# Attention then a three-way max feed-forward on one core: transposing one more group by DMA, moving copies and loads, spreading pieces, and cutting the last output tile

## The chip, the cores and the metric

The kernel runs on one core of a Trainium2 chip. The metric is the device time of one execution in microseconds (us). Runs of a kernel are compared by their medians.

The engines: PE (TensorE) multiplies matrices into PSUM; PEld is its loading of weights; DVE (VectorE), ACT (ScalarE) and POOL (GpSimd) work elementwise; SP (SyncE) issues DMAs. POOL issues DMAs too. Each engine executes its own instructions in order and waits on semaphores for the others.

## The reference

q, k, v are (8, 12, 448, 64) in float32: 8 batches, 12 heads, 448 tokens. The four weights are 768 x 768.

```python
scores = scale * np.matmul(q, k.transpose(0, 1, 3, 2))
m = np.max(scores, axis=-1, keepdims=True)
e = np.exp(scores - m)
attn = e / (np.sum(e, axis=-1, keepdims=True) + np.exp(-m) + 1e-09)
x = (attn @ v).transpose(0, 2, 1, 3).reshape(8 * 448, 768)
h = np.maximum(np.maximum(x @ w1, x @ w2), x @ w3)
out = h @ w_out                      # (3584, 768), float32
```

The kernel takes exp of the scaled scores without subtracting the maximum, which turns the extra term of the denominator into 1.

## The kernel before

**Groups.** The 12 heads of a batch are three groups of four heads, two pairs each: 24 groups i in all (line 88). Groups 0 to 2 (batch 0) are computed in two halves of the query columns, "E" (256) and "O" (192): parts n = 0 to 5 (lines 499 to 545). From group 3 on, the loop of line 556 takes a whole group in three visits.

**Scores and exp.** A group has seven units (line 249). `scores` (line 260) computes a unit as 64x64 matmuls into a buffer `stp` and has ACT write exp of it into `e_buf` (line 294). Visits take the units (0, 1), (2, 3) and (4, 5, 6). The buffers `stp`, the accumulators `avp` of attention times V, and, where the call says so, the PE transposes' output share the pool `ps_s`, which has three buffers used in turn (line 79). Feed-forward pieces use `ps_b`, two buffers.

**K and Q transposed.** Scores need K and Q with the head dimension on the partitions. Groups below `PE_QK` (line 55) are transposed by PE: `transpose_pe` (line 172) does one pair, 11 blocks of 128x128, and one copy for K and one or two for Q take them out of PSUM on the engines that the call names (AC is ACT, DV is DVE). Groups from `PE_QK` on are transposed by two crossbar DMAs (a DMA that transposes) on SP's queue (`transpose_dma`, line 207), at the start of group i - 2; then `shift_q` (line 216) on POOL moves half blocks with four copies. KT and QT have three buffers each, so the DMA for group i waits until the scores of group i - 3 are done.

**V and loads.** `load_qk` (line 91) and `load_v` (line 108) issue loads from POOL, which turn float32 into float16; the raw tiles have four buffers. `prep_v` (line 354) copies V into the layout of the matmul with three copies, on DVE or POOL. For groups below `PE_QK`, `load_qk` also clears two columns with DVE (line 98).

**Attention times V.** At visits 0 and 1 of group i, `av` (line 495) multiplies the exp of group i - 1 by V; DVE divides by the sum into `xn` (lines 341 to 352). `x_transpose_pe` or, from group 3 on, a crossbar DMA on SP (line 382) turns xn into `xT`.

**Feed-forward pieces.** A batch's feed-forward is a list of pieces: `up_piece` (line 392; one of three weights, one or two column blocks; DVE copies the first product into hT and takes the maximum with the next two) and `out_piece` (line 418; half the width of an output tile of 128 tokens, scaled by DVE; after the second half two DMAs on SP's queue write 64 rows each). Each piece has a cost in PE columns. `fill(cols)` (line 467) adds to a credit and emits pieces while the credit is positive. In the parts, `UPE` (line 493) is given at four places of parts 3 to 5; in the groups, `share(n)` (line 551) is the cost that is left over the visits until the next batch's pieces arrive, in equal parts.

**The end.** After the last group come its attention times V, a crossbar transpose of its x, the pieces that remain, and then the whole last batch's 26 pieces (lines 597 to 602).

Of the kernel before, what the change touches and what calls it, by code (L numbers as in the profile page):

```python
# [14 lines left out]
ts = bass.ts  # L15
# [6 lines left out]
def kernel(  # L22
# [29 lines left out]
    scale = 1.0 / math.sqrt(D)  # L52


    PE_QK = 6
    NEB = 2
    NV = 3

# [295 lines left out]
    def prep_v(i, eng):  # L354
        t = raw[i].pop("v")
        vx, vt = v_buf[i % NV], vt_buf[i % NV]
        eng.tensor_copy(out=vx[:, :, :, 0:D], in_=t[:, :, 1:4, :])  # L357
        t2 = t.rearrange("p (r h) t d -> p r h t d", r=NP)
        eng.tensor_copy(out=vt[0:HP, :, 0:D], in_=t2[0:HP, :, 0, 4, :])
        eng.tensor_copy(out=vt[HP:P, :, 0:D], in_=t2[HP:P, :, 1, 0, :])  # L360
# [50 lines left out]
        else:  # L411
            nc.vector.tensor_tensor(out=dst, in0=dst, in1=src, op=ALU.max)  # L412

    NH = 2
    NW = DM // NH
    order = (0, 2, 4, 6, 1, 3, 5)

    def out_piece(bp, t, nh):
        if nh == 0:
            outs[0] = out_pool.tile([128, DM], FP32, tag="o_sb", name="o_sb")  # L420
        o_sb = outs[0]
        op_ps = ps_b.tile([128, 512], FP32, tag="b", name="op_ps")
        for fc in range(NFC):
            nc.tensor.matmul(  # L424
                out=op_ps[:, 0:NW],
                lhsT=hT[bp][:, fc, ts(t, 128)],
                rhs=wout_sb[:, fc, ts(nh, NW)],
                start=(fc == 0),
                stop=(fc == NFC - 1),
            )  # L430
        nc.vector.tensor_scalar(  # L431
            out=o_sb[:, ts(nh, NW)],
            in0=op_ps[:, 0:NW],
            scalar1=1.0 / LAMBDA,
            scalar2=None,
            op0=ALU.mult,
        )
        if nh == NH - 1:
            for half in range(2):
                n = 2 * t + half  # L440
                b = 2 * bp + n // T
                rows = out[b * S : (b + 1) * S].rearrange("(p t) m -> t p m", t=T)
                nc.sync.dma_start(out=rows[order[n % T]], in_=o_sb[half * HP : half * HP + HP])


    UP = NDC * (S + 6)
    OUT = NFC * (NW + 6)
    pieces = []

    def add_up(b, q0, qn, order):  # L450
        w = 1 if qn == S else 2
        for i, f0 in order:
            fcs = tuple(range(f0, f0 + w))
            pieces.append((up_piece, (b, fcs, i, q0, qn), NDC * w * (qn + 6)))

    def add_out(b):
        for t in range(0, 3) if b % 2 == 0 else range(3, 7):
            for nh in range(NH):
                pieces.append((out_piece, (b // 2, t, nh), OUT))

    def add_batch(b):
        add_up(b, 0, S, [(i, fc) for fc in range(NFC) for i in range(3)])
# [27 lines left out]

    parts = [(part, g) for part in "EO" for g in range(NG)]
    PW = {"E": (0, 1), "O": (2, 3), "EO": (0, 1, 2, 3)}
    UPE = 9 * 2 * NDC * (NE + 6) / 12

    def av(i, ej, pr, part):
        av_tail(i, ej, pr, PW[part])
        av_main(i, ej, pr, PW[part])

    for n, (part, g) in enumerate(parts):
        ej = n % NEB  # L500
        pp, pg = parts[n - 1] if n > 0 else (None, None)
        step = UPE if n > 2 else 0
        nxt = g + 1 if part == "E" and g < NG - 1 else None
        scores(g, ej, (0, 1), part)
        if n != 3:
            scores(g, ej, (2, 3), part)
        if n > 0:
            av(pg, 1 - ej, 0, pp)
        if n > 1 and n != 4:
            x_transpose_pe(parts[n - 2][1], parts[n - 2][0])  # L510
        if n == 3:
            av(pg, 1 - ej, 1, pp)
            scores(g, ej, (2, 3), part)
        fill(step)
        if nxt is not None and n > 0:
            transpose_pe(nxt, 0, ps_b, AC, (DV,))
        fill(step)
        scores(g, ej, (4, 5), part)
        scores(g, ej, (6,), part)
        if n == 0:  # L520
            warm(4)
            transpose_pe(nxt, 0, ps_b, DV, (DV,))
        if n == 3:
            x_transpose_pe(pg, pp)
            add_up(0, 0, NE, [(i, f) for i in range(3) for f in (0, 2, 4)])
        if nxt is not None:
            transpose_pe(nxt, 1, ps_b, DV, (DV,))
        if n > 0 and n != 3:
            av(pg, 1 - ej, 1, pp)
        fill(step)  # L530
        if n == 5:
            transpose_pe(3, 1, ps_s, DV, (DV,))
        fill(step)
        if n == 0:
            prep_v(0, DV)
        if n == 1:
            load_weight(2)
        if n == 2:
            load_v(3)
            load_qk(4)  # L540
            load_weight(3)
        if n == 4:
            load_v(4)
            load_qk(5)
            transpose_pe(3, 0, ps_s, DV, (DV,))


    visits = ((0, 1), (2, 3), (4, 5, 6))
    adds = {3 * (3 * b + 4) + 1: b for b in range(1, B - 1)}

    def share(n):

        nxt = min([a for a in adds if a > n], default=3 * NI + 2)
        return left() / (nxt - n)

    for i in range(3, NI):
        ej, pj = (i + 1) % NEB, i % NEB
        first = i == 3
        if i + 2 < NI and i + 2 >= PE_QK:
            transpose_dma(i + 2)  # L560
        if first:
            load_v(5)
            load_qk(6)
        elif i + 2 < NI:
            load_v(i + 2)
            if i + 3 < NI:
                load_qk(i + 3)
        for vi, units in enumerate(visits):
            n = 3 * i + vi
            scores(i, ej, units)  # L570
            if vi < 2:
                av(i - 1, pj, vi, "O" if first else "EO")
            if vi == 1:
# [24 lines left out]
    av(NI - 1, NI % NEB, 1, "EO")  # L598
# [34 lines left out]
```

The softmax here doesn't subtract the row's maximum and nothing guards it: scores larger than these inputs give would overflow.

## Time and profile before

| | |
|---|---|
| median of 8 runs | 343.78 us (343.38 to 344.83) |
| the profiled execution | 343.93 us |
| its span, first to last instruction | 341.9 us |
| PE busy | 329.6 us, 96% of the span |
| DVE, ACT, POOL busy | 189.5, 146.4, 139.4 us |
| granted TensorE clock | 0.998 of full |
| DMA moved | 47.42 MB, mean 139 GB/s |

The span is cut into 40 slices of 8.5 us; a digit is the busy share in tenths:

```
PE   8889988999999999999999999999999999999993
ACT  2773366585444453544453543444453543300000
DMA  7999999999999999999995999979970460133006
```

A view of a stretch gives its length and then each engine's busy time with the number of instructions in brackets: PE, PEld, DVE, ACT, POOL, then the clock, DMA's mean busy share (over 1 where transfers overlap) and GB/s. A line of the timeline is start, length, engine, line of the code, operation, tiles, count, and in brackets the engine's idle time before it with what ended it. Matmuls overlap one another, so a matmul's length is not its cost; the chain of work that ended last gives the net times, and there six matmuls of 448 columns take 1.13 us. A view of DMA issues gives the time from issue to landing. SPq is SP's queue.

### The profile page before, as it was taken

How to read it: one execution, taken by the hardware profiler on the slowest of the kernel's cores; microseconds unless marked ns; L12 is line 12 of the kernel's file. 1: busy time of each engine (PE TensorE's matmuls, PEld its weight loads, DVE VectorE, ACT ScalarE, POOL GpSimd, SP SyncE). 2: the span in 40 equal slices, each digit the busy share in tenths (PEclk: the TensorE clock that was granted, in tenths of full speed). 3: DMA queues.
4: the chain of work that ended last, by engine and by line, in shares of the span. 5: the costliest groups of instructions: out<-in, count | busy, mean ns of one | idle time of the engine just before them, and what ended most of it. 6: DMA issues, size and time to landing. Idle time of an engine off the chain costs nothing.

```text
span 341.9 us, 9746 instructions
## 1 busy us (share of the span) xinstructions
PE 329.6 (96%) x4157; PEld 198.5 (58%) x4157; DVE 189.5 (55%) x418; ACT 146.4 (43%) x174; POOL 139.4 (41%) x247
## 2 busy tenths in 40 slices
PE   8889988999999999999999999999999999999993
PEld 4568767865545655555555655555556655465552
DVE  2565766655456466456556456556556555565552
ACT  2773366585544453543544453543544443300000
POOL 8693541917477172834355168164345000000000
PEclk9999999999999999999999999999999999999999
DMA  7999999999999999999995999979970460133006
GB/s 103 193 207 209 205 200 162 169 124 193 192 165 147 210 206 118 140 141 202 152 124 71 188 214 144 130 108 228 145 115 4 124 125 3 32 77 94 2 18 167
DMA packets 89499, 47.42 MB, mean 139 GB/s; under 512 B 58224, under 2 KB 85872, under 8 KB 89456
## 3 DMA queue, kind: packets, MB, share of 16 engines
q0 software_dynamic: 29392, 22.03, 47.2%
q1 hardware_dynamic: 60064, 24.78, 42.1%
q8 instruction: 32, 0.52, 0.6%
q14 instruction: 11, 0.09, 0.1%
HBM read 44.04 MB, written 11.01 MB: 161 GB/s over the span
## 4 chain that ended last, share of the span: by engine, by line
PE 92%; DVE 2%; ACT 2%; issue 1%; DMA 1%; POOL 0%; ACTq 0%; POOLq 0%
PE p_i L401 48%; PE op_ps L424 16%; PE avp L331 12%; PE stp L274 11%; PE avp L314 2%; PE trT L181 2%; ACT e L294 2%; DMA ld_k<-in_k_dram 1%; DVE QT L170 1%; DVE xn L347 0%; DVE xT L380 0%; PE xtp L374 0%; PE warm L155 0%; POOL ld_q L103 0%; DVE hT L412 0%
## 5 line engine op out<-in xcount | busy, mean ns | idle before, releaser
L294 ACT ACTIVATE e<-stp 128x896 f16<-128x896 f32 (+4 forms) x171 | 144.0, 903 | 144.5 <-PE stp L274 144.4
L401 PE MATMUL p_i<-xT,w 128*128 128x448 f16 (+2 forms) x972 | 173.6, 332 | 0.2
L401 PEld LDWEIGHTS <-w 128*128 128x128 f16 x972 | 89.8, 98 | 68.0 <-issue 5.3
L412 DVE TENSOR_TENSOR hT<-hT,p_i 128x448 f16<-128x448 f16 (+2 forms) x96 | 59.6, 621 | 43.4 <-PE p_i L401 43.2
L219 POOL COPY QT<-QT 64x384 f16<-64x384 f16 (+1 forms) x72 | 40.0, 556 | 101.8 <-DMA QT<-ld_q 80.5
L424 PE MATMUL op_ps<-w,hT 128*128 128x384 f16 x336 | 58.3, 326 | 0.0
L274 PE MATMUL stp<-QT,KT 64*64 64x448 f16 (+2 forms) x756 | 47.8, 338 | 3.4 <-ACT e L294 1.9
L331 PE MATMUL avp<-vx,e 128*128 128x65 f16 x1152 | 45.4, 193 | 0.0
L431 DVE TENSOR_SCALAR o_sb<-op_ps 128x384 f32<-128x384 f32 x56 | 31.0, 556 | 25.4 <-PE op_ps L424 22.4
L424 PEld LDWEIGHTS <-hT 128*128 128x128 f16 x336 | 31.6, 98 | 23.1 <-issue 2.1
L410 DVE CAST hT<-p_i 128x448 f16<-128x448 f32 (+2 forms) x48 | 30.0, 624 | 23.8 <-PE p_i L401 23.6
L331 PEld LDWEIGHTS <-e 128*128 128x128 f16 x1152 | 38.8, 97 | 2.3
L347 DVE TENSOR_TENSOR xn<-avp,rb 128x512 f16<-128x512 f32 (+1 forms) x54 | 34.1, 632 | 1.9
L274 PEld LDWEIGHTS <-KT 64*64 64x64 f16 x756 | 15.8, 105 | 28.2 <-issue 24.2
L341 DVE TENSOR_SCALAR rb<-avp 128x8 f32<-128x8 f32 (+1 forms) x54 | 9.0, 166 | 40.1 <-PE avp L331 40.0
L314 PEld LDWEIGHTS <-e 64*64 64x64 f16 x768 | 14.5, 107 | 9.2 <-DVE QT L170 0.8
L103 POOL DMA_DIRECT2D ld_q<-in_q_dram x24 | 17.7, 737 | 4.1 <-PE avp L331 1.6
L103 POOL DMA_DIRECT2D ld_k<-in_k_dram x25 | 17.9, 716 | 3.2 <-DMA w<-in_moe_w_out_dram 1.5
L357 POOL COPY vx<-ld_v 128x768 f16<-128x768 f16 x20 | 16.4, 819 | 5.2 <-issue 2.7
L314 PE MATMUL avp<-vt,e 64*64 64x65 f16 x768 | 15.7, 193 | 1.4 <-DVE QT L170 0.6
L116 POOL DMA_DIRECT2D ld_v<-in_v_dram x24 | 15.2, 633 | 3.1 <-DMA ld_q<-in_q_dram 1.9
L113 POOL DMA_DIRECT2D ld_v<-in_v_dram x24 | 15.2, 635 | 2.3 <-DVE rb L341 1.6
(33 smaller groups left out, 85.1 us busy)
## 6 DMA issues: line engine op xcount, KB each, us to landing
out_dram<-o_sb SPq DMA_DIRECT2D x56, 192.0 KB, 3.3
ld_v<-in_v_dram POOLq DMA_DIRECT2D x48, 128.0 KB, 5.0
ld_q<-in_q_dram POOLq DMA_DIRECT2D x24, 224.0 KB, 7.5
ld_k<-in_k_dram POOLq DMA_DIRECT2D x23, 224.0 KB, 6.9
w<-in_moe_w_dram POOLq DMA_DIRECT2D x9, 384.0 KB, 9.2
w<-in_moe_w_out_dram POOLq DMA_DIRECT2D x3, 384.0 KB, 10.9
xT<-xn SPq DMA_TRANSPOSE x21, 4.9
QT<-ld_q SPq DMA_TRANSPOSE x18, 6.0
```

Of the source, the lines that this page charges most:

```text
L103: nc.gpsimd.dma_start(out=tiles[nm][:, 1 : NP * T + 1].rearrange("x (r t) d -> x r (t d)", r=NP)[:, p0:p1], in_=src[:, p0:p1],)
L219: eng.tensor_copy(out=t[d0 : d0 + HP, o * 128 : (o + n) * 128], in_=t[s0 : s0 + HP, a * 128 : (a + n) * 128],)
L274: nc.tensor.matmul(out=stp[half * HP : half * HP + HP, par, j * qn : (j + 1) * qn], lhsT=k_block(i, pr, h2, x[half]), rhs=q_cols(i, pr, h2 ...
L294: nc.scalar.activation(out=dst, in_=src, func=AF.Exp, scale=scale)
L314: nc.tensor.matmul(out=ps[half * HP : half * HP + HP, hh, j * D1 : (j + 1) * D1], lhsT=eF[hh * HP : hh * HP + HP, o : o + HP], rhs=vt[hh * ...
L331: nc.tensor.matmul(out=ps[:, hh, j * D1 : (j + 1) * D1], lhsT=eF[:, o : o + 128], rhs=vx[:, 2 * pr + hh, (x[0]), 0:D1], start=False, stop= ...
L347: nc.vector.tensor_tensor(out=xn[i][:, pr, ws[0] : ws[0] + nw].rearrange("p j h d -> p h j d"), in0=acc[:, :, :, 0:D], in1=rb[:, :, 0:nw]. ...
L401: nc.tensor.matmul(out=p_i[:, j * qn : (j + 1) * qn], lhsT=w_sb[i][:, dc, ts(fc, 128)], rhs=xT[b][:, dc, q0 : q0 + qn], start=(dc == 0), s ...
L410: nc.vector.tensor_copy(out=dst, in_=src)
L412: nc.vector.tensor_tensor(out=dst, in0=dst, in1=src, op=ALU.max)
L424: nc.tensor.matmul(out=op_ps[:, 0:NW], lhsT=hT[bp][:, fc, ts(t, 128)], rhs=wout_sb[:, fc, ts(nh, NW)], start=(fc == 0), stop=(fc == NFC - 1),)
L431: nc.vector.tensor_scalar(out=o_sb[:, ts(nh, NW)], in0=op_ps[:, 0:NW], scalar1=1.0 / LAMBDA, scalar2=None, op0=ALU.mult,)
```

## The change

1. `PE_QK` goes from 6 to 5: group 5 is transposed by DMA, shifted by POOL, and its V is copied by POOL.
2. Parts: `UPE` is one whole piece of 3144 columns instead of 2358; it is given once after `add_up` in part 3 and twice each in parts 4 and 5, instead of four times in each. V of group 0 is copied by DVE before the second transpose of part 0 instead of at its end; that transpose's Q is copied out by ACT and DVE. The transposes of group 3 have Q copied out by ACT instead of DVE, and the one in part 5 stands before the `fill`.
3. Groups: the transposes of group 4 stand at visits 0 and 1 of group 3, before the `fill`, and are copied out by ACT; before, they stood at visits 1 and 2 in the middle of the `fill`, copied by DVE.
4. POOL's V copies are those of group i + 1 and stand at the end of group i, ahead of `shift_q(i + 2)`; before, they were those of group i and stood in visit 1. The loads of V for group i + 3 and K, Q for group i + 4 stand at the end of group i behind `shift_q`, from group 4 on; before, V of i + 2 and K, Q of i + 3 stood at the start of group i.
5. `share` counts 2200 columns for attention times V at visits 0 and 1, so that these get fewer pieces and visit 2 more.
6. The last output tile is written as columns of 384, 256 and 128, each with its own two DMAs: both on SP, both on ACT, and one on each.

```diff
-    PE_QK = 6
+    PE_QK = 5
...
-    def out_piece(bp, t, nh):
-        if nh == 0:
+    def out_piece(bp, t, c, w, queues):
+
+        if c == 0:
             outs[0] = out_pool.tile([128, DM], FP32, tag="o_sb", name="o_sb")
+            outs[1] = 0
...
-        if nh == NH - 1:
-            for half in range(2):
...
-                nc.sync.dma_start(out=rows[order[n % T]], in_=o_sb[half * HP : half * HP + HP])
+        if queues is None:
+            return
+        for half in range(2):
...
+            queues[half].dma_start(
+                out=rows[:, outs[1] : c + w], in_=o_sb[half * HP : half * HP + HP, outs[1] : c + w]
+            )
+        outs[1] = c + w
...
     def add_out(b):
+        sy, sc = nc.sync, nc.scalar
         for t in range(0, 3) if b % 2 == 0 else range(3, 7):
-            for nh in range(NH):
-                pieces.append((out_piece, (b // 2, t, nh), OUT))
+            cuts = [(0, NW, None), (NW, NW, (sy, sy))]
+            if b == B - 1 and t == 6:
+                cuts = [(0, NW, (sy, sy)), (NW, 256, (sc, sc)), (NW + 256, 128, (sy, sc))]
+            for c, w, queues in cuts:
+                pieces.append((out_piece, (b // 2, t, c, w, queues), NFC * (w + 6)))
...
-    UPE = 9 * 2 * NDC * (NE + 6) / 12
+    UPE = 2 * NDC * (NE + 6)
...
-        step = UPE if n > 2 else 0
+        step = UPE if n > 3 else 0
...
             transpose_pe(nxt, 0, ps_b, AC, (DV,))
-        fill(step)
         scores(g, ej, (4, 5), part)
         scores(g, ej, (6,), part)
         if n == 0:
             warm(4)
             transpose_pe(nxt, 0, ps_b, DV, (DV,))
+            prep_v(0, DV)
         if n == 3:
             x_transpose_pe(pg, pp)
             add_up(0, 0, NE, [(i, f) for i in range(3) for f in (0, 2, 4)])
+            fill(UPE)
         if nxt is not None:
-            transpose_pe(nxt, 1, ps_b, DV, (DV,))
+            transpose_pe(nxt, 1, ps_b, DV, (AC, DV) if n == 0 else (DV,))
         if n > 0 and n != 3:
             av(pg, 1 - ej, 1, pp)
+        if n == 5:
+            transpose_pe(3, 1, ps_s, DV, (AC,))
         fill(step)
-        if n == 5:
-            transpose_pe(3, 1, ps_s, DV, (DV,))
-        fill(step)
-        if n == 0:
-            prep_v(0, DV)
...
-            transpose_pe(3, 0, ps_s, DV, (DV,))
+            transpose_pe(3, 0, ps_s, DV, (AC,))
...
+    AVC = 2200
+
     def share(n):
...
-        return left() / (nxt - n)
+        rest = range(n, nxt)
+        sums = [AVC if m % 3 < 2 and m < 3 * NI else 0 for m in rest]
+        return max(0, (left() + sum(sums)) / len(rest) - sums[0])
...
-        if first:
-            load_v(5)
-            load_qk(6)
-        elif i + 2 < NI:
-            load_v(i + 2)
-            if i + 3 < NI:
-                load_qk(i + 3)
+        def loads(iv, iq):
+            if iv < NI:
+                load_v(iv)
+            if iq < NI:
+                load_qk(iq)
+
+        if i < 5:
+            loads(i + 2, i + 3)
...
             if vi == 1:
-                prep_v(i, nc.vector if i < PE_QK else nc.gpsimd)
+                if i < PE_QK:
+                    prep_v(i, nc.vector)
...
-            if vi > 0 and i + 1 < PE_QK:
-                fill(per / 2)
-                transpose_pe(i + 1, vi - 1, ps_s, DV, (DV,))
-                fill(per / 2)
-            else:
-                fill(per)
-        if i + 2 < NI and i + 2 >= PE_QK:
+            if vi < 2 and i + 1 < PE_QK:
+                transpose_pe(i + 1, vi, ps_s, AC, (AC,))
+            fill(per)
+        if PE_QK <= i + 1 < NI:
+            prep_v(i + 1, nc.gpsimd)
+        if PE_QK <= i + 2 < NI:
             shift_q(i + 2, nc.gpsimd)
+        if i >= 4:
+            loads(i + 3, i + 4)
```

More of the change, by code (lines that the diff above doesn't have):

```diff
@@ L412, in up_piece @@
             nc.vector.tensor_tensor(out=dst, in0=dst, in1=src, op=ALU.max)
-    NH = 2
-    NW = DM // NH
+    NW = DM // 2
     order = (0, 2, 4, 6, 1, 3, 5)
-    def out_piece(bp, t, nh):
-        if nh == 0:
+    def out_piece(bp, t, c, w, queues):
+        if c == 0:
             outs[0] = out_pool.tile([128, DM], FP32, tag="o_sb", name="o_sb")
+            outs[1] = 0
         o_sb = outs[0]
@@ L424, in out_piece @@
             nc.tensor.matmul(
-                out=op_ps[:, 0:NW],
+                out=op_ps[:, 0:w],
                 lhsT=hT[bp][:, fc, ts(t, 128)],
-                rhs=wout_sb[:, fc, ts(nh, NW)],
+                rhs=wout_sb[:, fc, c : c + w],
                 start=(fc == 0),
@@ L431, in out_piece @@
         nc.vector.tensor_scalar(
[L432 to L435, printed above, removed]
+            out=o_sb[:, c : c + w], in0=op_ps[:, 0:w], scalar1=1.0 / LAMBDA, scalar2=None,
             op0=ALU.mult,
         )
-        if nh == NH - 1:
-            for half in range(2):
-                n = 2 * t + half
-                b = 2 * bp + n // T
-                rows = out[b * S : (b + 1) * S].rearrange("(p t) m -> t p m", t=T)
-                nc.sync.dma_start(out=rows[order[n % T]], in_=o_sb[half * HP : half * HP + HP])
+        if queues is None:
+            return
+        for half in range(2):
+            n = 2 * t + half
+            b = 2 * bp + n // T
+            rows = out[b * S : (b + 1) * S].rearrange("(p t) m -> t p m", t=T)[order[n % T]]
+            queues[half].dma_start(
+                out=rows[:, outs[1] : c + w], in_=o_sb[half * HP : half * HP + HP, outs[1] : c + w]
+            )
+        outs[1] = c + w
     UP = NDC * (S + 6)
-    OUT = NFC * (NW + 6)
     pieces = []
```

## The prediction

> **What bounds the kernel now.** I read the page's busy shares first, then TensorE's (PE) busy time stage by stage, then its waits in order of time.
>
> ```profile
> PE 329.6 (96%) x4157; PEld 198.5 (58%) x4157; DVE 189.5 (55%) x418; ACT 146.4 (43%) x174; POOL 139.4 (41%) x247
> 60.00:100.00 40.00, 40.00 (x608) 25.34 (x606) 23.20 (x52) 23.81 (x29) 23.32 (x42) 1.00 1.23 168
> 34.56:42.03 7.47, 6.88 (x122) 5.79 (x120) 5.12 (x15) 2.71 (x4) 4.04 (x7) 1.00 1.24 204
> 42.03:51.85 9.82, 8.44 (x135) 6.73 (x134) 6.48 (x18) 5.99 (x7) 4.49 (x7) 1.00 1.30 201
> 51.85:61.90 10.05, 9.16 (x181) 7.83 (x180) 6.64 (x18) 5.99 (x7) 3.42 (x7) 1.00 1.25 157
> ```
>
> The last four are a stretch, its length, then PE's busy time. From 60 us on PE has no idle time up to its last matmul near 336.7, so spreading pieces differently there can win nothing: only work taken from PE, idle time before 62 us, and the 5.2 us behind the last matmul can shrink. Group 3 (42.03 to 51.85) has 1.38 us of idle PE, group 4 0.89.
>
> The timeline names the waits; brackets hold the idle time and its releaser:
>
> ```profile
> 46.07 0.33 PE L181 MATMUL trT<-ident,ld_k 128*128 128x128 f16 x3 [0.35 <-ACT e L294]
> 48.34 0.38 PE L274 MATMUL stp<-QT,KT 64*64 64x448 f16 x4 [0.89 <-ACT e L294]
> 58.88 0.38 PE L274 MATMUL stp<-QT,KT 64*64 64x448 f16 x4 [0.89 <-ACT e L294]
> 35.68 0.26 PE L314 MATMUL avp<-vt,e 64*64 64x65 f16 x8 [0.59 <-DVE QT L170]
> ```
>
> The first three have one cause: a group's PE transposes take one of the three `ps_s` buffers just before the visit that wants all three, so its third score unit waits for an exp. They are 2.13 us.
>
> **The change part by part.**
>
> *Group 5 leaves PE (PE_QK 6 to 5).* The chain of waits has each of its two transpose steps (56.87 and 60.36) as "0.61 PE trT L181 x11". Removed: 2 x 0.61 = 1.22 us, in a stretch where PE otherwise works: full gain. DVE also loses four copies. Added are two crossbar transposes on SP's queue and four shift copies on POOL (2.38 us), priced below.
>
> The Trainium skill (VectorE: DVE Perf Modes, "The three transpose paths" and its rules) speaks against this: TensorE if PSUM will do, 390 ns a 128x128 block against 1309 ns for the crossbar. The trace pays 0.61/11 = 55 ns a block on PE and 5.3 us to land a Q transpose of seven blocks. By the page's figure, as an estimate, that would land after 9.2 us and group 5 would be about 3 us late, which would eat most of the change's gain.
>
> *Transposes of group 4 at visits 0 and 1, copied out by ACT.* That removes 0.35 and 0.89 in group 3; group 4, with no PE transposes left, loses its 0.89. ACT takes over four copies in two visits of group 3: K 0.49 and 0.60 (its rows for 384 and 512 columns), Q of 1024 and 896 columns. ACT's Q copy of that width is not shown; ends are 0.60 (512 columns) and 1.03 (its 1024-wide exp); I take 1.0 and 0.9, the nearer row by width. So ACT has 6.4 us of exps plus 3.0 in group 3, 9.4 against about 10.8 of PE (below): covered, but behind the visit-1 exp the second transpose waits about 0.3. Net 2.13 - 0.3 = **1.8 us**; ends 1.0 (ACT's order bites each time) and 2.1.
>
> *Fewer pieces early.* Before, parts 3, 4, 5 run 2, 3, 3 pieces of 1.31 us (rows of 12 matmuls in the chain); now 1, 2, 2, then 1, 1, 2 in group 3. Parts keep 3.3 to 5.6 us of PE work against 2.9 us of exps, so the cover holds and the three pieces move, costing nothing. If it failed, each part would show some 0.5 us of wait. The 0.59 at 35.68 stays: the Q copy before it goes from DVE (0.68) to ACT (1.0), but starts without K's 0.29 ahead.
>
> *V copy ahead at part 0.* DVE's V copies (13.67 to 14.44) move ahead of the last K/Q copies; V landed near 11.5 (issued 5.15 and 5.78, landing 6.0), so nothing new waits. The av matmul at 14.27, which waits for them, comes 0.1 earlier, and score unit 3 0.2 later: 0.1 gained, ends -0.3 and +0.3.
>
> *Loads and POOL's order.* Laid side by side, POOL's order from group 6 on is the same cycle (loads, V copy, shift copies); only the V copy is of the next group. Loads "two groups ahead" stand where they stood. What is new is group 5's shift copies ahead of V6 and QK7's loads. POOL executes in order, so those loads wait for the crossbar transpose of Q5:
>
> ```profile
> 39.09 0.71 POOL L103 DMA_DIRECT2D ld_q<-in_q_dram  x1 [0.40 <-PE avp L331]
> 46.96 0.63 POOL L113 DMA_DIRECT2D ld_v<-in_v_dram  x1 [0.40 <-issue]
> 52.88 1.32 SPq L211 DMA_TRANSPOSE QT<-ld_q  x1
> 54.32 1.65 SPq L211 DMA_TRANSPOSE KT<-ld_k  x1
> 58.32 2.38 POOL L219 COPY QT<-QT 64x384 f16<-64x384 f16 x4 [7.91 <-DMA QT<-ld_q]
> 60.64 0.62 POOL L113 DMA_DIRECT2D ld_v<-in_v_dram  x1
> 70.02 1.50 SPq L211 DMA_TRANSPOSE QT<-ld_q  x1
> ```
>
> Q5 is issued at 39.09 and lands 10.1 us later, 49.2. Its transpose, like that of 52.88, takes 5.3: 54.5. Shift copies end at 56.9; K5's transpose (6.8 at 54.32) ends by 57.4. Group 5's scores come at 61.90 - 1.22 - 1.83 - 0.1 and less one odd piece of 0.99 = **57.8**: in time by half a microsecond. V6 is then issued at 56.9, not 46.96. In before, V7's issue at 60.64 led to Q8's landing at 70.0 (62.56 + 7.4), 9.4 later; so Q7 lands at 65.5 to 66.3. Its transpose takes 5.3 to 7.7 (rows at 52.88 and 70.02): 70.8 to 74.0, shift copies to 73.2 to 76.4; K7's 1.5 later by 6.8 to 8.5. Group 7's scores come at 77.34 - 3.15 = **74.2**. So a wait of 0 to 2.2; I take **0.6**, from the middle of the transposes' rows. Group 8 (shift end before 80.2, scores 87.84) keeps over 3 us, and later groups more.
>
> *V copies of POOL* (0.82 + 0.29 + 0.29): one group earlier, V landed a cycle before; nothing waits. Group 5's moves from DVE to POOL.
>
> *Spreading by AVC.* PE is full there: 0. The bigger remainder at the end (about 19,900 columns, 8.3 us, before 7.5) still covers the last x transpose (2.8 us).
>
> *The end.*
>
> ```profile
> 336.78 0.56 DVE L431 TENSOR_SCALAR o_sb<-op_ps 128x384 f32<-128x384 f32 x1 [0.42 <-PE op_ps L424]
> out_dram<-o_sb SPq DMA_DIRECT2D x56, 192.0 KB, 3.3
> ```
>
> The last matmul ends at T = 336.74. Now: scaling 0.56, two issues on SP at 0.57, landing 2.6 for the last two: T + 3.76. Then 1.4 us to the span's end. After: the 256-column scaling ends near T + 0.13 (0.56 for 384 columns and 0.17 for 8 give 0.42 and, for 128, 0.29). ACT issues its two DMAs, then one of the last two; the third starts at T + 0.17 + 2 x 0.52 = T + 1.2. ACT issues no DMA in this trace; by SP's rows one takes 0.47 to 1.03. Landing of 32 KB is not shown: between 1.8 (2.6 less 0.8, for the 192 KB fewer in flight at the tail's some 230 GB/s) and 2.6; I take 2.2: T + 3.4. **0.35 gained**; ends -1.0 (issues of 1.03) and +1.2 (issues of 0.3, landing 1.8). The extra matmuls cost nothing: 6 x 55 ns and 6 x 109 sum to the 0.97 of one old piece.
>
> The Trainium skill (DMA: Bandwidth & Descriptors, "Rules for kernel authors") calls transfers under 64 KB mostly overhead, and more issuing engines a saving of issue time alone. By its fit (2.0 us plus bytes at 436 GB/s, an estimate) 32 KB lands in 2.1 against 2.45 for 192 KB, a landing gain of 0.35, near my 0.4; the trace's 2.6 agrees with the larger.
>
> *Sum:* 1.22 + 1.83 + 0.1 + 0.35 - 0.6 = **2.9 us**. The profiled execution took 343.93 (span 341.9 plus 2.0): 341.0. It lies 0.15 above the median 343.78, so **340.9**.
>
> **Rivals.**
> 1. *The waits return as ACT waits.* ACT at 9.4 of 10.8 us delays exps instead. For: 0.35 at 46.07 already is ACT. Against: ACT is at 5.99 in both stretches and idles. Gain 1.22 + 0.35 (the end), no wait at group 7 since PE is later: 342.2.
> 2. *Group 7 long late.* The transposes take 7.7 and 8.5 as at 70.02, wait 2.2, perhaps 0.5 at group 5. For: DMA's mean busy share is 1.2 to 1.3 until 77 us. Against: a transpose at 59.30 landed in 3.4. 342.5 to 343.1.
> 3. *Slower than before.* The same chain, POOL held by group 5's shift copies: shift 7 ends at 56.8 plus three landings (Q5's transpose, Q7's load counted from its issue, Q7's transpose). It is in time up to 17.4; from 17.4 + 3.5 + 0.7 = 21.6 the kernel is slower. With three of the long rows, 9.4 + 8.0 + 9.4 = 26.8, 9.4 late: about 349.7. Against: with loads held back, fewer transfers compete just then.
> 4. *It doesn't do what it says.* The load move alone is no new order on POOL; if the PE gain is also eaten by waits of 2 to 4 us, no change: 343.8.
>
> **How the numbers follow.** Forecast 0.55, its own range 339.5 to 341.8 (wait 0 to 1.2, the end's middle ends); rival 1 0.15; rival 2 0.17; rival 3 0.05; rival 4 0.08. Best end: 1.22 + 2.1 + 0.3 + 1.0 = 4.6, 339.2; the high end takes in rivals 1 and 2: 343.1. Faster by over 0.2% (0.7 us, about what a measurement can tell) holds the first three: 0.87; within it 0.08; slower 0.05.
>
> **What would show it.** In the profile after, trT has 22 PE transposes fewer; no 0.89 waits on ACT between 38 and 60 us; a POOL shift copy near 54.5 and V6's issue behind it near 57; any PE wait at group 7's first scores (near 74) with the release by POOL's shift copy or DMA KT; last matmul to span end near 4.8 instead of 5.2. Wrong would be: waits on ACT in parts 3 to 5, or a wait at group 5's scores over 0.5 us.

## The result and the profile after

The changed kernel takes **349.4 us** (median of 11 runs, 345.77 to 351.63), the kernel before 343.89 us beside it (32 runs, 343.31 to 345.31): a ratio of 1.0136, 95% interval 1.0115 to 1.0157. It is slower by 5.5 us, where 2.9 us of gain were forecast. Ratios here and below leave disturbed executions out, so they can differ a little from the quotients of the medians. The profiled execution took 347.93 us; its span is 346.1.

The page of the changed kernel: the busy line, and the chain that ended last by engine and by line.

```profile
PE 330.2 (95%) x4141; PEld 198.3 (57%) x4141; DVE 185.0 (53%) x405; ACT 151.3 (44%) x181; POOL 142.9 (41%) x254
...
PE 87%; DMA 5%; ACT 3%; DVE 3%; issue 1%; SPq 0%; ACTq 0%
PE p_i L401 47%; PE op_ps L425 14%; PE avp L331 10%; PE stp L274 10%; DMA KT<-ld_k 3%; ACT e L294 2%; DMA xT<-xn 2%; PE avp L314 2%; PE trT L181 2%; PE warm L155 2%; ACT QT L168 1%; DVE hT L410 0%; DVE QT L170 0%; DVE xn L347 0%; DVE xT L380 0%
```

PE did 22 transposes less (1.22 us), yet it is busy for longer (330.2, before 329.6): some of its work ran more slowly. And two DMA steps, "KT<-ld_k" and "xT<-xn", stand on the chain. PE's waits (total, times, longest) name them:

```profile
PE p_i L401 <- DMA xT<-xn: 3.1, 1, 3.1
PE stp L274 <- DMA KT<-ld_k: 1.2, 1, 1.2
...
```

PE's timeline of the changed kernel puts these and the longer of the early waits in order of time:

```profile
33.17 0.26 PE L314 MATMUL avp<-vt,e 64*64 64x65 f16 x8 [1.05 <-ACT QT L168]
48.63 1.47 PE L401 MATMUL p_i<-xT,w 128*128 128x256 f16 x12 [0.56 <-DVE hT L412]
58.52 1.15 PE L401 MATMUL p_i<-xT,w 128*128 128x192 f16 x12 [0.69 <-DVE hT L410]
77.27 0.57 PE L274 MATMUL stp<-QT,KT 64*64 64x448 f16 x8 [1.24 <-DMA KT<-ld_k]
85.10 3.00 PE L401 MATMUL p_i<-xT,w 128*128 128x448 f16 x8 [3.06 <-DMA xT<-xn]
```

The 0.35, 0.89, 0.89 and 0.59 of before (2.72 us) have become 1.05, 0.35, 0.35, 0.56 and 0.69 (3.00 us): other waits, no fewer. Group 7's scores wait 1.24 for K, where 0.6 was forecast. The largest wait is a new one: batch 1's first feed-forward pieces wait 3.06 for group 5's x transpose. They then take 3.00 for eight matmuls, twice the usual. The windows of 2 us there (length, then busy time and instructions of PE, PEld, DVE, ACT, POOL; the third figure from the end is PE's granted clock) say why:

```profile
82.00:84.00 2.00, 0.04 (x1) 0.00 (x0) 0.45 (x1) 0.00 (x0) 1.84 (x4) 1.00 1.31 190
84.00:86.00 2.00, 0.90 (x3) 0.39 (x3) 0.11 (x1) 0.00 (x0) 2.00 (x5) 0.82 1.20 261
86.00:88.00 2.00, 2.00 (x6) 0.61 (x4) 0.52 (x1) 0.00 (x0) 1.90 (x4) 0.50 1.13 321
88.00:90.00 2.00, 2.00 (x19) 0.89 (x19) 0.62 (x1) 1.27 (x2) 0.12 (x1) 0.83 1.36 206
90.00:92.00 2.00, 2.00 (x12) 1.06 (x11) 1.11 (x2) 1.26 (x2) 0.00 (x0) 1.00 1.23 198
```

Behind the wait the clock is at half for (0.18 + 0.50 + 0.17) x 2 / 0.5 = 3.4 us, which costs 1.7 us of work. Of the 4.0 us between the two profiled executions that makes: 1.24 + 3.06 + 1.7 lost, 0.3 lost in the early waits, 1.22 won on the transposes and, in this execution, 0.75 at the end (last matmul to span's end 4.4, before 5.16): 4.3, within 0.3 of it. In the other runs the time roughly follows the mean clock too: 345.77 at 0.999, 348.55 at 0.993, 350.95 at 0.988. Even the first of them, with hardly any fall of the clock, is 1.9 us above the kernel before.

Why is x late? SP's queue (issues of transposes and output DMAs), the changed kernel:

```profile
65.41 1.22 SPq L211 DMA_TRANSPOSE QT<-ld_q  x1
66.69 3.44 SPq L211 DMA_TRANSPOSE KT<-ld_k  x1
70.18 3.58 SPq L384 DMA_TRANSPOSE xT<-xn  x1
75.27 1.53 SPq L211 DMA_TRANSPOSE QT<-ld_q  x1
76.90 1.24 SPq L211 DMA_TRANSPOSE KT<-ld_k  x1
78.24 1.26 SPq L384 DMA_TRANSPOSE xT<-xn  x1
```

The same queue before, behind the transpose of Q8 at 70.02:

```profile
71.56 4.11 SPq L211 DMA_TRANSPOSE KT<-ld_k  x1
75.77 1.18 SPq L443 DMA_DIRECT2D out_dram<-o_sb  x2
77.04 2.12 SPq L384 DMA_TRANSPOSE xT<-xn  x1
```

POOL in the changed kernel:

```profile
55.42 2.40 POOL L219 COPY QT<-QT 64x384 f16<-64x384 f16 x4 [8.75 <-DVE rb L341]
57.77 0.63 POOL L113 DMA_DIRECT2D ld_v<-in_v_dram  x1
...
66.17 0.74 POOL L103 DMA_DIRECT2D ld_q<-in_q_dram  x1
```

The landing of the x transpose (the last figure, us from issue), before and in the changed kernel:

```profile
xT<-xn SPq DMA_TRANSPOSE x1, 4.9
xT<-xn SPq DMA_TRANSPOSE x1, 6.8
```

Read from POOL's view upward: POOL issues the loads of V6 and group 7 only behind group 5's shift copies (57.77, before 46.96), and these wait for group 5's transposes (Q5's lands near 54.9; the last half microsecond to 55.42 the profile puts down to DVE); the loads of group 8 end with Q8 at 66.17, which lands near 75.2. SP executes in order, and Q8's transpose (75.27) has to wait for that load; group 5's x transpose, whose xn DVE has ready at 72.5, stands behind it, goes out at 78.24 and lands after 6.8, at 85.06. Before, it went out at 77.04, landed after 4.9 at 81.9, and the matmuls that need it (the fifth and sixth of a piece that begins at 81.34 in the chain) were due near 82.1: a margin of 0.2 us. So of the 3.1 us by which x lands later, 1.2 are a later issue and 1.9 a longer way from issue to landing.

### The profile page after: what moved, and what is told of

The parts are those of the page before. It is cut to its first block, busy times and chain, and to the rows that moved or that the text cites. A ratio compares the mean times of both kernels' runs of the same rounds, so it can differ in the third digit from the quotient of the medians.

```text
span 346.1 us, 9759 instructions
## 1 busy us (share of the span) xinstructions
PE 330.2 (95%) x4141; PEld 198.3 (57%) x4141; DVE 185.0 (53%) x405; ACT 151.3 (44%) x181; POOL 142.9 (41%) x254
## 3 DMA queue, kind: packets, MB, share of 16 engines
q1 hardware_dynamic: 62000, 25.08, 42.2%
## 4 chain that ended last, share of the span: by engine, by line
PE 87%; DMA 5%; ACT 3%; DVE 3%; issue 1%; SPq 0%; ACTq 0%
PE p_i L401 47%; PE op_ps L425 14%; PE avp L331 10%; PE stp L274 10%; DMA KT<-ld_k 3%; ACT e L294 2%; DMA xT<-xn 2%; PE avp L314 2%; PE trT L181 2%; PE warm L155 2%; ACT QT L168 1%; DVE hT L410 0%; DVE QT L170 0%; DVE xn L347 0%; DVE xT L380 0%
## 5 line engine op out<-in xcount | busy, mean ns | idle before, releaser
L219 POOL COPY QT<-QT 64x384 f16<-64x384 f16 (+1 forms) x76 | 42.3, 556 | 103.0 <-DMA QT<-ld_q 71.6
L425 PE MATMUL op_ps<-w,hT 128*128 128x384 f16 (+2 forms) x342 | 58.3, 323 | 0.0
L432 DVE TENSOR_SCALAR o_sb<-op_ps 128x384 f32<-128x384 f32 (+2 forms) x57 | 31.2, 549 | 24.9 <-PE op_ps L425 23.2
L274 PEld LDWEIGHTS <-KT 64*64 64x64 f16 x756 | 15.7, 105 | 27.9 <-issue 21.6
L357 POOL COPY vx<-ld_v 128x768 f16<-128x768 f16 x21 | 17.2, 819 | 6.3 <-issue 3.7
```

Source lines behind the costliest of these rows:

```text
L219: eng.tensor_copy(out=t[d0 : d0 + HP, o * 128 : (o + n) * 128], in_=t[s0 : s0 + HP, a * 128 : (a + n) * 128],)
L274: nc.tensor.matmul(out=stp[half * HP : half * HP + HP, par, j * qn : (j + 1) * qn], lhsT=k_block(i, pr, h2, x[half]), rhs=q_cols(i, pr, h2 ...
L425: nc.tensor.matmul(out=op_ps[:, 0:w], lhsT=hT[bp][:, fc, ts(t, 128)], rhs=wout_sb[:, fc, c : c + w], start=(fc == 0), stop=(fc == NFC - 1),)
L432: nc.vector.tensor_scalar(out=o_sb[:, c : c + w], in0=op_ps[:, 0:w], scalar1=1.0 / LAMBDA, scalar2=None, op0=ALU.mult,)
```

## The experiments

My theory after the traces: **the change makes loads and transposes late, and SP's order passes this lateness on to x; the clock adds to it.** Rivals: it is the early waits; the held loads alone; the added transfers alone; the new order of V, K and Q.

**1. Which part of the change?** `a_qk6` is the changed kernel with all but part 1, `b_qk5` the kernel before with part 1 alone.

```diff
a_qk6, on the changed kernel        b_qk5, on the kernel before
-    PE_QK = 5                      -    PE_QK = 6
+    PE_QK = 6                      +    PE_QK = 5
```

> The changed kernel with group 5 again transposed by PE (PE_QK back to 6); all else as changed. Theory A (group 5's crossbar transposes and shift copies hold POOL, so the loads of groups 6 and 7 start 11 us late, group 7's KT and then group 5's xT come late, and PE's clock falls behind the long wait): no PE wait on a DMA between 70 and 90 us, clock 1.0 there, and with nothing gained from the moved copies but 0.75 us at the end, 342.5 to 343.7 us. Theory B (the moved copies, pieces and loads cost the time, whatever transposes group 5): still 347 us or more.

> The kernel before with one edit alone: PE_QK 5. Theory A: the same holding of POOL, so waits on KT of group 7 and on xT of group 5 of some 3 to 5 us together, less 1.2 us of PE transposes, plus 1 to 2 us at a lower clock: 346 to 350 us. Theory B: the edit alone gains its 1.2 us: 342.6 us.

Measured: `a_qk6` 343.37 us, ratio 0.9995 (0.9984 to 1.0006); `b_qk5` 347.98, 1.0129 (1.0110 to 1.0148). PE's timeline of `b_qk5`:

```profile
78.39 0.66 PE L314 MATMUL avp<-vt,e 64*64 64x65 f16 x16 [2.47 <-POOL vt L359]
85.87 2.81 PE L401 MATMUL p_i<-xT,w 128*128 128x448 f16 x14 [1.24 <-DMA xT<-xn]
```

So the loss is group 5's move to DMA; the rest of the change, spread pieces and tail with it, is worth nothing that can be measured. In the old order POOL's V copy stands behind shift copies and loads, and PE waits 2.47 for it. The changed kernel has no such wait, which I put down to its earlier V copies. `b_qk5` also shows that x can be late without a late issue: there it goes out at 76.64, ahead of the 77.04 of before, and lands after 9.2.

**2. The loads back in their old place.** `c_loads_first` is the changed kernel with V6 and group 7 loaded ahead of group 5's shift copies.

```diff
-        if i < 5:
-            loads(i + 2, i + 3)
+        if i == 3:
+            loads(5, 6)
+            loads(6, 7)
```

> The changed kernel with the loads of V6 and K, Q of 7 issued ahead of group 5's shift copies (both sets of loads at the start of group 3). Theory A: POOL issues them near 47 us instead of 57.8, KT of group 7 lands some 6 us earlier and the 1.2 us wait goes; T8 is no longer late, so the 3.1 us wait on xT of group 5 shrinks to 1 us or less and the clock stays up: 341 to 343 us. A variant of A (SP's order alone makes xT late, since it stands behind group 8's transposes): the xT wait stays above 2 us, 345 us or more. Theory B: 347 us or more.

Measured: 348.82 us, 1.0142 (1.0106 to 1.0178): no gain, against theory A. POOL's timeline:

```profile
48.00 0.63 POOL L113 DMA_DIRECT2D ld_v<-in_v_dram  x1 [0.53 <-issue]
48.62 0.62 POOL L116 DMA_DIRECT2D ld_v<-in_v_dram  x1
49.34 0.71 POOL L103 DMA_DIRECT2D ld_k<-in_k_dram  x1
59.23 0.70 POOL L103 DMA_DIRECT2D ld_q<-in_q_dram  x1 [9.19 <-DMA QT<-ld_q]
```

V6 and K7 go out early, Q7 does not: its issue waits for the crossbar transpose of Q5, which with more transfers beside it takes 8.7 us. Group 5's shift copies, now behind Q7 on POOL, start at 59.98 and not 55.42, and PE waits for them at group 5's scores; a stretch at half clock follows (windows of 2 us as above):

```profile
60.53 0.38 PE L274 MATMUL stp<-QT,KT 64*64 64x448 f16 x2 [1.36 <-POOL QT L219]
61.20 0.57 PE L274 MATMUL stp<-QT,KT 64*64 64x448 f16 x6 [0.29 <-POOL QT L219]
62.00:64.00 2.00, 2.00 (x34) 1.90 (x31) 1.06 (x3) 1.40 (x2) 1.82 (x5) 0.67 0.88 160
64.00:66.00 2.00, 2.00 (x35) 1.23 (x34) 0.55 (x1) 0.79 (x1) 1.84 (x4) 0.50 0.15 21
66.00:68.00 2.00, 2.00 (x41) 1.69 (x42) 1.15 (x4) 0.94 (x2) 2.00 (x4) 0.97 0.82 133
```

Then all of POOL is late again (Q8 is issued at 68.13, its transpose at 79.53), and PE waits 2.7 for x (at 86.56). This run moved three of four issues and put a new wait ahead of them, so it does not show what early loads would be worth.

**3. Each suspect alone, on the kernel before.** `x_dma_only` adds group 5's two crossbar transposes, into tiles that nothing reads (PE still transposes group 5). `y_hold_only` adds no DMA, but holds the loads of V6 and group 7 back behind a copy of group 3's xn, and adds two V-sized copies on POOL behind them.

```diff
x_dma_only, at the start of i = 3, ahead of its loads:
+            for j, nm in enumerate("qk"):
+                nc.sync.dma_start_transpose(out=scr[j]..., in_=raw[5][nm]...)
y_hold_only, in visit 1 of i = 4, in place of the loads at its start:
+                if i == 4:
+                    nc.gpsimd.tensor_copy(out=scr[2][:, 0, 0, :], in_=xn[3][:, 1, 0, 0, :])
+                    load_v(6)
+                    load_qk(7)
+                    for j in range(2):
+                        nc.gpsimd.tensor_copy(out=scr[j], in_=raw[5]["v"][:, :, 1:4, :])
```

> The kernel before with group 5's two crossbar transposes issued as an extra at the start of group 3, into a buffer that nobody reads; PE still transposes group 5 and POOL waits for nothing new. It adds only work for the DMA engines: by the queue's share (143.9 us of all 16 engines before, 146.8 in the changed kernel) some 2.9 us. Theory C (the DMA engines are full until batch 1 starts, xT of group 5 lands without margin, and their added work is paid by PE as a wait plus a lower clock): a PE wait on xT or on KT before 90 us of 1 to 4 us, 345.5 to 350 us. Theory A (POOL held is the cause): 343.5 to 344.2 us, no wait.

> The kernel before with POOL held and no DMA work added: the loads of V6 and K, Q of 7 wait behind a small copy of group 3's xn (ready near 57 us) and two copies of 0.82 us follow them, as the V copy does in the changed kernel. Theory A: K and Q of 7 land near 65 us and not 57, T7 and T8 are late, PE waits on KT of group 7 or xT of group 5: 345.5 to 350 us. Theory C: the loads are late by some microseconds, but nothing is added: below 344.5 us. Both above 345 would say that each is enough by itself.

Measured: `x_dma_only` 347.05 us, 1.0094 (1.0062 to 1.0126); `y_hold_only` 351.23, 1.0163 (1.0074 to 1.0253), a loss larger than the range given for it. Both stop at the same matmul as the changed kernel; PE's timeline of `x_dma_only`, then of `y_hold_only`:

```profile
85.14 4.49 PE L403 MATMUL p_i<-xT,w 128*128 128x448 f16 x14 [2.86 <-DMA xT<-xn]
```

```profile
85.92 5.09 PE L403 MATMUL p_i<-xT,w 128*128 128x448 f16 x14 [4.17 <-DMA xT<-xn]
```

In both, Q8's transpose goes out late on SP (75.89 and 74.64, before 70.02) and x behind it (79.93 and 79.72, before 77.04). So each of the two is enough by itself, and neither is needed for a loss of this kind.

**4. SP's order.** Three kernels move transposes of K and Q behind the x transpose on SP, all of them on the changed kernel: `d_xt_first` for every group from 6 on, `d2_xt_before_t8` from 8 on, `d3_xt_before_t8_once` for group 8 alone. A fourth, `e_qk_before_v`, leaves SP as it is and loads K and Q ahead of V instead, to bring group 7's and 8's transposes forward.

```diff
d3_xt_before_t8_once
-        if i + 2 < NI and i + 2 >= PE_QK:
+        if i + 2 < NI and i + 2 >= PE_QK and i != 6:
             transpose_dma(i + 2)
...
                     x_transpose_dma(i - 1)
+                    if i == 6:
+                        transpose_dma(8)
e_qk_before_v
         def loads(iv, iq):
-            if iv < NI:
-                load_v(iv)
             if iq < NI:
                 load_qk(iq)
+            if iv < NI:
+                load_v(iv)
```

> The changed kernel with SP's order altered: from group 4 on the crossbar transposes of group i + 2 are issued behind the x transpose of group i - 1 and not ahead of it. Theory A with SP's order as its second link: xT of group 5 is issued near 73 us and not 78, the 3.1 us wait and the fall of the clock go, the wait on KT of group 7 (1.2 us) stays: 342.5 to 344 us. If the x transpose is late by the DMA engines' load and not by its place: no change, 347 to 350 us.

> The changed kernel with the crossbar transposes of group i + 2 behind the x transpose of group i - 1 on SP only from group 6 on, so that T6 and T7 keep their place (moving T6 too had cost a 2.6 us wait on KT of group 6). Theory A with SP's order as second link: xT of group 5 is issued near 73 us, in time for batch 1's first pieces; the 1.2 us wait on KT of group 7 stays; the clock stays up: 342.5 to 344.5 us. If x is late by the DMA engines' load: 347 us or more.

> The changed kernel with one pair moved on SP: group 8's crossbar transposes behind the x transpose of group 5, everything else in its place (moving the later ones too had let output DMAs wait behind transposes and gave two waits of 2.4 us near 122 and 204 us). If SP's order at this one place turns the late loads into the 3.1 us wait: no wait on xT of group 5, clock at 1.0, 342.5 to 344 us. If not: 347 or more.

> The changed kernel with K and Q of a group loaded ahead of the V of the group before it; POOL is held as before until Q5's transpose lands. Theory A (group 7's K and Q come late because POOL is held): they are issued 1.2 us earlier and no V load is ahead of them on the DMA engines, so T7 starts some 2 to 3 us earlier, the 1.2 us wait on KT of group 7 goes and the 3.1 us wait on xT of group 5 shrinks by 2 or more: 343 to 346 us. If the DMA engines' load as a whole decides, whatever order the loads have: no change, 347 to 350 us.

Measured: `d_xt_first` 346.87 us, 1.0054 (1.0017 to 1.0090); `d2_xt_before_t8` 348.62, 1.0142 (1.0104 to 1.0180); **`d3_xt_before_t8_once` 343.15, 0.9980 (0.9954 to 1.0007)**; `e_qk_before_v` 349.22, 1.0132 (1.0101 to 1.0164). Of the three that move transposes only the last came out as expected. The wait for x near 85 us is gone in all three, but in the first two another comes: PE's timeline of `d_xt_first`, where group 6's transposes were moved too and land late,

```profile
69.11 0.57 PE L274 MATMUL stp<-QT,KT 64*64 64x448 f16 x8 [2.56 <-DMA KT<-ld_k]
```

of `d2_xt_before_t8`, where output DMAs now stand on SP behind transposes that wait,

```profile
122.40 4.11 PE L401 MATMUL p_i<-xT,w 128*128 128x448 f16 x12 [2.41 <-DVE o_sb L432]
```

and of `d3_xt_before_t8_once`, where between 70 and 90 us only group 7's K is left, with the clock at 1.00 throughout:

```profile
77.45 0.57 PE L274 MATMUL stp<-QT,KT 64*64 64x448 f16 x8 [1.63 <-DMA KT<-ld_k]
```

Ahead of group 8's transposes, x goes out on SP at 74.06 and lands after 4.9, near 79.0:

```profile
74.06 2.75 SPq L384 DMA_TRANSPOSE xT<-xn  x1
```

So one pair of issues in another order is worth 5.4 us of the changed kernel by the ratios (6.2 by the medians), with x issued 4.2 us earlier and 1.9 us less on its way. In `e_qk_before_v` group 7's wait goes, PE comes 1.9 us earlier to batch 1's pieces, and x, still behind group 8, is late by more:

```profile
76.27 4.81 SPq L384 DMA_TRANSPOSE xT<-xn  x1
85.85 3.15 PE L401 MATMUL p_i<-xT,w 128*128 128x448 f16 x8 [5.66 <-DMA xT<-xn]
```

Its time is that of the rival (the DMA engines' load decides), and x is issued earlier than in the kernel before (76.27, before 77.04) but lands after 9.5. So it is not the issue alone that counts: behind group 8's transposes x can also take longer to land. These runs don't separate the two, since the swap changes both.

**5. Is SP's order the last link everywhere?** The swap of `d3` on the two kernels of experiment 3, and on the kernel before as their control.

> The kernel before with group 5's two crossbar transposes added (their output unused; 347.05 by themselves), and group 8's transposes behind group 5's x transpose on SP. My theory (SP's order is the last link): the wait of 2.9 on xT goes and the time falls to that of before plus at most 1: 343.6 to 344.8. Rival (the added transfers delay xT itself, or other waits take its place): over 346.

> The kernel before with V6's and group 7's loads held back (351.23 by themselves), and group 8's transposes behind group 5's x transpose on SP. My theory: the wait of 4.2 on xT goes; a wait on group 7's K or shift copies may stay (up to 2 us): 343.6 to 346. Rival (loads held back delay all that follows, whatever SP's order): over 348.

> The kernel before with only group 8's transposes behind group 5's x transpose on SP. No wait stands there in before, so no change is expected by either theory: 343.5 to 344.2. Were it faster by over 0.7, the mended versions of the change would owe that to the order alone.

Measured: `z_before_swap` 343.98 us, 0.9998 (0.9981 to 1.0015), so the order wins nothing where nothing is late. `x2_dma_swap` 346.65, 1.0076 (1.0058 to 1.0093); `y2_hold_swap` 350.3, 1.0143 (1.0095 to 1.0191). Both hardly better than without the swap: my expectation missed. The wait for x did go, but the lateness comes out at the next place; PE's timeline of `x2_dma_swap`:

```profile
90.26 0.66 PE L316 MATMUL avp<-vt,e 64*64 64x65 f16 x16 [2.01 <-POOL vt L361]
```

It is the kind of V copy that `b_qk5` waits for in experiment 1, late behind shift copies and loads on POOL. `y2_hold_swap` waits 0.92 and 1.03 for the same copy in the execution profiled, which took 346.45 us; its other runs took 350.1 and more, and I have no trace that says why. So SP's order is the last link in the changed kernel and not in the order of before. That the changed kernel owes this to its earlier V copies fits the wait, but no run moves them alone.

**6. The clock.** `f_warm` is the changed kernel with 15 matmuls of zeros (3.2 us) just ahead of batch 1's first piece, into a tile that nothing reads.

```diff
                 if adds[n] == 1:
+                    warm(15)
```

> The changed kernel with 15 matmuls of zeros (3.2 us of PE work that nobody reads) ahead of batch 1's first piece, where PE waits 3.1 us for xT of group 5. If the fall of the granted clock behind that wait (0.50 to 0.83 between 84 and 90 us) is a second cost of the wait itself, PE stays busy, the clock stays at 1.0 there, and the kernel becomes faster by doing more: 345.5 to 347 us. If the clock's fall is not tied to PE's idle time: 349 to 351 us.

Measured: 347.1 us, 1.0103 (1.0076 to 1.0129). The median is 2.3 us below the changed kernel's with more work on PE, but the interval overlaps that of the changed kernel (1.0115 to 1.0157), so a gain is not shown. The execution profiled took 349.08, the longest of the four. PE's timeline:

```profile
80.64 3.40 PE L155 MATMUL warm<-wz 128*128 128x512 f16 x15
83.88 0.92 PE L401 MATMUL p_i<-xT,w 128*128 128x448 f16 x4
87.82 1.67 PE L401 MATMUL p_i<-xT,w 128*128 128x448 f16 x8 [3.02 <-DMA xT<-xn]
```

The eight matmuls take 1.67 instead of 3.00, and the clock is 1.00 in every window from 66 to 92 us. But PE still waits 3.02 for x, as long as in the changed kernel: x, issued at 77.42, takes 10.4 to land, and this later arrival (87.8, in the changed kernel 85.06) costs more than the 1.7 that the clock saves. The run shows that a wait of this length can pass without a fall of the clock; it does not show that filling PE's idle time prevents the fall.

**7. The early waits and the end.** `i_qk6_dve` is `a_qk6` with group 3's Q copied by DVE again, against the 1.05 on ACT. `g_tail_only` is the kernel before with part 6 of the change alone.

```diff
i_qk6_dve, on a_qk6
-            transpose_pe(3, 1, ps_s, DV, (AC,))
+            transpose_pe(3, 1, ps_s, DV, (DV,))
...
-            transpose_pe(3, 0, ps_s, DV, (AC,))
+            transpose_pe(3, 0, ps_s, DV, (DV,))
```

> The changed kernel with PE_QK 6 (343.4 us) and group 3's Q copied out by DVE again and not by ACT. In its profile PE waits 1.05 us at 32.8 us for ACT's Q copy and 0.34 at 36.3 for an exp; before, DVE's copy gave one wait of 0.59. If the ACT copies are what ate the gain of the moved transposes: 0.5 to 0.8 us less, 342.6 to 342.9 us. If these waits only move: 343.4 us.

> The kernel before with the last output tile alone cut into 384, 256 and 128 columns on SP's and ACT's queues. By the changed kernel's profile (4.4 us from the last matmul to the span's end, 5.2 before): 343.0 us, 0.7 less than before. If the second queue or the extra DMAs cost as much outside the span: 343.7, no change.

Measured: `i_qk6_dve` 344.08 us, 1.0003 (0.9990 to 1.0015); `g_tail_only` 343.85, 1.0001 (0.9989 to 1.0012). PE's waits of `i_qk6_dve`:

```profile
PE avp L314 <- DVE QT L170: 0.6, 1, 0.6
```

The 1.05 has become 0.6, as DVE's copy had it before, and the time is no better. Its profile has two waits for loads, at different places of PE's timeline:

```profile
6.26 0.34 PE L181 MATMUL trT<-ident,ld_k 128*128 128x128 f16 x3 [1.07 <-DMA ld_k<-in_k_dram]
40.94 0.62 PE L181 MATMUL trT<-ident,ld_q 128*128 128x128 f16 x8 [0.77 <-DMA ld_q<-in_q_dram]
```

The first lies ahead of the edit and can't come from it (in `a_qk6` it is 0.51). The second lies behind it: PE begins this transpose step at 39.83 (39.77 in `a_qk6`) and then stands until Q of group 4 arrives. That the early part is bound by such arrivals is a reading; no run here shows it. In the end of `g_tail_only` the three DMAs on ACT take

```profile
336.93 2.01 ACTq L443 DMA_DIRECT2D out_dram<-o_sb  x3
```

0.67 each to issue, the last data lands near 340.0, and 1.9 us follow to the span's end instead of 1.4.

**8. Both mends together.** `j_d3_qk_before_v` is the changed kernel with the swap of `d3` and the loads of `e_qk_before_v`.

> The changed kernel with two orders mended: group 8's crossbar transposes stand behind group 5's x transpose on SP, and K and Q are loaded ahead of V. My theory (late loads cost a wait on group 7's K, and SP's order turns the lateness into a wait and a loss of clock at batch 1's first pieces): no wait on KT at 77 us and at most 1 us on xT, so 1.2 to 1.6 below the 343.15 of the kernel with the first mend alone: 341.5 to 342.3. Rival (the early part is bound by arrivals, and what is saved comes back as a wait on xT or on V): 343 to 344.5, with such a wait in the profile.

Measured: **342.41 us, 0.9960 (0.9929 to 0.9991)**, the only kernel of the study below the kernel before by its interval. Its runs spread from 341.36 to 346.36. PE's timeline of the execution profiled (344.34 us):

```profile
82.37 1.67 PE L401 MATMUL p_i<-xT,w 128*128 128x448 f16 x8 [1.99 <-DMA xT<-xn]
```

Group 7's wait is gone and part of it is back as a wait for x, as the rival had it, without a fall of the clock. The median lies between the ranges of theory and rival and decides for neither. Against `d3` (0.9954 to 1.0007) the step is not shown to win anything.

## Why the prediction was wrong

- **Group 5 leaves PE, 1.22:** right. 22 transposes fewer, and group 5's scores come at 59.59, against 61.90 - 1.22 - 0.99 (the moved piece) = 59.69. That also leaves nothing for the three waits.
- **Three waits, 1.8:** wrong, measured about nothing (2.72 before, 3.00 after; `a_qk6` 0.9995, `i_qk6_dve` 1.0003). The waits on ACT's exps at the scores did go, as said, and came back at other releasers: the Q copy on ACT (1.05 where I kept 0.59), DVE behind pieces (0.56 and 0.69). ACT's Q copies took 1.02 and 0.92, as I had them, but the one at 32.10 began behind DVE's copy of K, which I had left out of its way. I took a wait's length as gain without asking what PE reaches next; my first rival had the direction.
- **Fewer pieces cover the exps:** waits of the size that I named for its failure came (0.56 and 0.69), in groups 3 and 4 and not in the parts, and at DVE instead of ACT. The 0.69 also shows a neighbour that I left out: DVE's V copies at 56.13 took 0.67, 0.59 and 0.52 beside POOL's shift copies, and 0.35, 0.18 and 0.19 without them.
- **The chain behind the held loads:** right as far as I followed it. Q5's transpose was issued at 49.19 (49.2 forecast), V6 at 57.77 (56.9), Q7's transpose at 65.41 (65.5 to 66.3). Group 7's transposes took 9.6 and 10.5 us where I had 5.3 to 7.7 and 6.8 to 8.5; the wait was 1.24 where I took 0.6 and had a range to 2.2. My estimate of 9.2 us by the Trainium skill's figure for the crossbar (VectorE: DVE Perf Modes, "The three transpose paths") was nearer here; for Q5 it was not (5.7; I had 5.3 by the row before).
- **"Group 8 … keeps over 3 us, and later groups more":** this is the step that failed. I followed group 8's chain to its own scores and stopped; the sum has no term for what stands behind its transposes on SP. Group 8's scores indeed never waited (its shift copies ended at 84.07, its scores began at 93.67). But its transposes hold SP until Q8 has landed, and group 5's x transpose, with a margin of 0.2 us, stands behind them: a wait of 3.06 at batch 1's first pieces, and a clock at half behind it. `d3_xt_before_t8_once` shows it with one reordering (349.4 to 343.15, ratio 1.0136 to 0.9980), so all of the loss against the kernel before hangs on this place. The 2.2 us that `d3` still lacks to the 340.9 of the forecast are about what the three waits (1.8) and the end (0.35) had promised.
- **The clock:** not in the sum at all. 1.7 us for one wait, by the windows; the slower runs have a lower mean clock still.
- **The end, 0.35:** not seen (1.0001, 0.9989 to 1.0012). ACT's issues took 0.67 each where I took 0.52, and behind the last landing, 1.9 us followed where I had 1.4. The fit of the Trainium skill (DMA: Bandwidth & Descriptors, "Anatomy of one DMA — SWDGE (gpsimd) path") that I set beside it is given there for DMAs issued from GpSimd; these go out from SP and ACT, and their 32 KB landed after 2.3 and 2.2 in `g_tail_only`, where I took 2.2.
- **The third rival** had the right mechanism, POOL held by group 5's shift copies. Its three landings measured 5.7 + 5.6 + 9.6 = 20.9, short of the 21.6 from which it would decide, and it looked for the loss at group 7's scores. At that place the kernel lost only 1.24. That its 349.7 lies near the measured 349.4 is luck.

What stays open: how x's lateness divides between its later issue and its longer way to landing; how much of the loss in the slowest runs of the changed kernel (to 350.95) is more stretches at half clock; why `y2_hold_swap` mostly takes over 350 us; and what early loads of group 7 are worth, as `c_loads_first` did not bring Q7 early.

## What to carry to other kernels

When something is made late on an in-order queue, follow every later instruction of that queue to its own consumer, not only the data that is late; the thin margin may be that of an unrelated transfer behind it. Count a removed wait as gain only if what comes next on the engine is already there: here the early waits moved and the time did not. And try the smallest reordering: the same swap won nothing back when done from group 8 on (1.0142) and took back the loss when done once (0.9980).

## What the runs showed of the hardware

- **PE's clock fell in whole stretches of 3.4 us.** Worked out of windows as above, the clock was 0.50 for 3.4 us after waits of 2.34 and 2.41 (`d2_xt_before_t8`), 2.47 (`b_qk5`), 2.56 (`d_xt_first`), 2.7 (`c_loads_first`), 2.86 (`x_dma_only`) and 3.06 (after). It was 0.50 for twice that, 6.8, around 4.17 (`y_hold_only`) and 5.66 (`e_qk_before_v`), where the stretch began within the wait (near 83.8 and 83.5), so that only 2.3 and 2.2 us of work were lost. After 1.24, 1.37, 1.63, 1.99 and 2.01 the clock stayed at 1.00, and also after the 3.02 of `f_warm`; but in `c_loads_first` a whole stretch, 62.9 to 66.3, follows waits of only 1.36 and 0.29. So the length of a wait does not decide alone, and no threshold comes out of these runs. Where a stretch followed a wait of 2.3 to 3.1 us, it cost 1.7 us more than the wait itself. The Trainium skill (TensorE: Matmul & The Clock Gate, "What's actually happening") has a free-running window of about 3.4 us, which fits the length of the stretches and would leave room for exceptions like these two; its advice to keep gaps under some 3 us ("Why this matters for your kernels") is too wide here.
- **Crossbar transposes with loads in flight** landed after 9.6 and 10.5 us (Q7 and K7 in the changed kernel, issued at 65.41 and 66.69 among group 8's loads) and 10.7 (group 6's K in `d_xt_first`). Q6 and K6 in the changed kernel, issued at 52.74 and 54.57 with no load issued between 46.67 and 57.77, landed after 3.8 and 3.5. Two transposes more took some 2.8 us more of 16 engines' time on the hardware queues (42.1% of 341.9 before; 42.2% and 0.2% of 346.1 after).
- **A load's issue waited for a transpose that it shares no data with:** by the profile's releaser, Q7's for Q5's, 9.19 us in `c_loads_first`, though Q7's raw tile is that of group 3, which PE transposes. No run here shows why.
